# Pairs of units with one f and one scan, PSUM banks named one by one, and another order of issue in a recurrence-plus-highway kernel

## The chip, the core and the metric

The kernel runs on one core of one Trainium2 chip. The metric is the device time of one execution in microseconds (us). The core has a matrix engine (PE, with its weight loads PEld), a vector engine (DVE), a scalar engine (ACT), a GpSimd engine (POOL) and a sync engine (SP), which here issues nearly all transfers. Each engine works through its own queue in program order. PE writes only to PSUM, which has 8 banks of 512 fp32 columns; DVE and ACT read PSUM, POOL does not.

## What is computed

Four sequences of 6336 tokens with 256 features pass through a gated recurrence; the result of all 25344 tokens then passes through a highway layer.

```
sig = 1 / (1 + exp(-f_logit))
f = lower_bound + (1 - lower_bound) * sig
i = 1 - f
h = 0                                  # for each of the 4 sequences
for t in range(6336):
    h = f[:, t] * h + i[:, t] * x[:, t]
    y[:, t] = h

H = max(y @ w_h, 0)
T = 1 / (1 + exp(-(y @ w_t + b_t)))
out = T * H + (1 - T) * y
```

Inputs and output are fp32; the two input arrays and the output are 25.95 MB each.

## The kernel before

The tokens are cut into 28 units of whole blocks of 128 tokens (`parts`, L42): two units of 2 blocks, one of 4, twenty-three of 8, one of 4, one of 2. Features are two halves of 128 (`h`, `m`). For each unit the steps are these; the letter is the one used in the order.

- `l`, `x` (L235): load logits and x, up to 1 MB each, tokens on partitions.
- `u` (L247, ACT): u = sigmoid(-logits), 2048 columns for a unit of 8 blocks. The gate is f = 1 - (1 - lower_bound) u.
- `b` (L255, POOL, or DVE where the token ends in `v`): products u times x in bf16, in two pieces of 1024 columns.
- `i` (L262, PE): transposes of u, 8 of 128 columns, so that features lie on partitions and time along the columns; `f` (L273 on ACT, L271 on DVE): the gate, read from PSUM.
- `p` (L282, PE): transposes of the products, two bf16 values as one fp32 word; `s` (L299, DVE): the scan along time, y = f*y + b, which reads the products in PSUM and carries on from the last column of the unit before. A scan is cut where a sequence begins.
- `z`, `g` (L311 and, without a new weight load, L113; PE): the two matrix products, in pieces of 512 columns. The weights are scaled by 1 - lower_bound, because the scan leaves that factor out.
- `t` (L324, ACT): the sigmoid of z; `d` (L328, DVE): max(g, -(1 - lower_bound) y); `e` (L334, POOL or DVE): d = d * t.
- `o` (L347 and L348, PE): y times a diagonal plus d, transposed back to tokens on partitions, 4 blocks at a time; `c` (L357 on ACT, L355 on DVE): the copy from PSUM; `w` (L362): the store of 512 KB.

Once at the start come the loads of the weights (`wt`, `wh`), the small parameters (`pc`, `cc`, `dg`) and the scaling of the weights (`WT`, `WH`, DVE). `k*16` and `k*4` are matmuls on zeros whose result nobody reads (L124, L113).

The string `order` (L48 to L97) sets the order of everything: each token calls one of the functions, and instructions keep that order on each engine and in the queue of each engine, SP's included. The number behind the colon names the buffer. PSUM is cut into two buffers of one bank (`a0`, `a1`: uT and bT) and three of two banks (`b0` to `b2`: z, g, op). SBUF has six buffers for `l`, six for `x`, four each for `u`, `f`, `y`, `d` and `o`, three for `t` and `bv`. A transfer waits on SP until its buffer is free or its data is there, and the transfers behind it wait with it. `shared` (L176) makes the first POOL step behind a DVE step of the kind `b`, `e`, `dg`, `WT` or `WH` wait for that DVE step.

Of the kernel before, what the change touches and what calls it, by code (L numbers as in the profile page):

```python
# [11 lines left out]
FP32 = mybir.dt.float32  # L12
# [7 lines left out]
def kernel(  # L20
# [10 lines left out]
    nc = tc.nc  # L31
# [10 lines left out]
    parts = [2] * 2 + [4] + [8] * 23 + [4] + [2]  # L42
    units, at = [], 0
    for nb in parts:
        units.append((nb, at, {2: (0, 1), 4: (0, 1, 2), 8: (0, 2, 4)}[nb], {2: (0, 256, 512), 4: (0, 512, 1024), 8: (0, 1024, 2048)}[nb]))
        at += nb * P
    assert at == B * S
    order = """  # L48
l0:0 l1:1 x0:0 l2:2 wh wt x2:1 x1:2 u0:0 l3:3 pc:0 u2:1 x3:3 cc u1:2 l4:0 i0.1:0 x4:4 dg b0.0v:0 i0.0:1 k*16:1 l5:4
f0.0v:0 x5:5 f0.1v:1 WH p0.0:0 WT p0.1:1 k*4:0 s0.1:0 l6:5 x6:0 i2.0:1 b1.0:0 s0.0 f2.0:1 i1.0:0 z0.1:0 f1.0v:0 g0.1:1  # L50
g0.0:2 d0.1:0 b2.0:1 d0.0 p1.1:1 t0.1:0 i1.1:0 z0.0:0 k*4:1 b2.1 f1.1v:2 s1.1:1 p1.0:0 t0.0 p2.0:1 s1.0 e0.0 s2.0:2
z1.1:0 e0.1 u3:0 i2.1:0 z1.0:1 g1.1:2 b3.0:0 d1.1:1 p2.1:1 f2.1:0 g1.0:2 s2.1 t1.0:0 b3.1v d1.0 i3.0:0 k*4:1 t1.1
f3.0:1 g2.0:0 o0.0:1 i3.1:0 e1.1 e1.0 u4:1 d2.0:0 f3.1:0 p3.0:1 c0.0:0 s3.0:0 b4.1:1 z2.1:2 k*4:0 o1.0:0 b4.0 p3.1:0
# [19 lines left out]
f16.0:2 b16.1:1 l19:0 d13.1 b16.0 t13.0 p15.0:1 c12.0:2 i17.1:0 x19:3 f17.1:1 z14.1:1 g14.0:0 p15.1:0 e13.1 s15.0:2
o12.1:2 b17.1:0 u18:2 d14.0:0 z14.0:0 p16.0:1 b17.0 l20:1 t14.1:1 t14.0 c12.1:0 s15.1 g14.1:1 i16.1:0 s16.0:1 z15.0:0
f16.1:0 e13.0v w12.0 z15.1:2 d14.1 e14.0 t15.0:2 p16.1:0 i17.0:1 e14.1 w12.1 t15.1 o13.0:0 b18.1:1 f17.0:2 c13.0:1
w13.0 l21:2 x20:0 u19:0 g15.0:2 s16.1 b18.0 p17.0:1 d15.0:1 o13.1:1 g16.0:0 i18.1:0 c13.1:3 z16.1:2 g15.1:1 f18.1:0
s17.0:3 w13.1 t16.1:0 i19.1:0 d16.0:2 p17.1:1 f19.1:2 o14.0:2 u20:1 o14.1:0 b19.0:0 l23:0 c14.1:0 i18.0:0 w14.1 b19.1
# [12 lines left out]
x27:3 o22.0:2 t23.1:1 b26.0:0 s24.1 e21.0v t21.1 c22.0:1 z23.0:0 p25.0:0 e21.1 o22.1:1 t23.0 z24.1:2 u27:0 i26.0:1  # L90
g24.0:0 s25.0:0 c22.1:2 f26.0:0 b26.1 z24.0:1 d24.0:0 p25.1:1 t24.1:2 i26.1:0 w20.1 e23.0 t24.0 o21.0:2 e23.1 g24.1:0
f26.1:1 c21.0:0 e24.0 o21.1:1 s25.1 p26.0:0 c21.1:3 p26.1:1 d24.1 s26.1:3 z25.1:2 w22.0 t25.1:0 g25.1:0 w22.1 w21.0
d25.1:1 o23.0:1 w21.1 s26.0 o23.1:2 i27.1:1 c23.0:1 z25.0:0 b27.0:0 w23.0 c23.1:0 g26.0:1 g25.0:2 t25.0 e24.1v d26.0:2
d25.0 i27.0:0 e25.1 e25.0v w23.1 f27.0:0 z26.1:0 o24.0:1 f27.1:1 p27.0:0 p27.1:1 z26.0:2 s27.0:2 s27.1 t26.1:1 c24.0:2
o25.0:0 t26.0 g26.1:1 w24.0 o24.1:2 d26.1 z27.0:1 c24.1v:0 c25.0:1 t27.0:0 o25.1:0 c25.1:3 e26.0 g27.0:1 d27.0:0 e26.1
o26.0:2 w25.0 w24.1 z27.1:1 t27.1 e27.0v c26.0:2 w25.1 w26.0 g27.1:0 d27.1 e27.1v o27.0:0 c27.0:1 w27.0
"""  # L97

    NU = len(units)
# [3 lines left out]
    st = [dict() for _ in range(NU)]  # L103
# [15 lines left out]
    extra = [0]  # L119

    def busy(t):
        for k in range(extra[0]):
            if k == 0:
                pin(nc.tensor.matmul(t[:, :512], zeros[:, :P], zeros, start=True, stop=True))  # L124
            else:
                pin(again(t[:, :512], zeros[:, :P], zeros, True, True))

    def one_bank(slot, dtype, name):
        t = ps.tile([P, NB * P], dtype, tag=f"a{slot}", name=name)
        busy(t.bitcast(FP32))  # L130
        return t

    def two_banks(slot, name):
        t = ps.tile([P, NB * P], FP32, tag=f"b{slot}", name=name)
        busy(t)
        return t
# [13 lines left out]
    for _ in range(8):  # L150
        nc.tensor.matmul(once["idle"][:, :512], zeros[:, :P], zeros, start=True, stop=True)
# [251 lines left out]
```

## Time and profile before

| what | value |
|---|---|
| runs | 213.06, 212.94, 210.38 us; median 212.94 |
| the profiled execution, span of its instructions | 209.0 us |
| transferred | 78.67 MB, mean 376 GB/s |
| ACT, POOL busy | 191.1 us (91%), 176.2 us (84%) |
| last load of x issued on SP | at 174.40 us |
| SP's own waiting | 130.2 us for ACT copies, in 42 waits |

The profile gives a span from the first to the last instruction of one execution; the time of the runs has 1.4 to 4.1 us beside such a span. Busy times are unions of instruction records, and neighbouring records on DVE and ACT overlap by some 0.1 us, so start-to-start distances are the better price of one more or one less instruction. A matmul's record is longer than the distance to the next matmul, since matmuls are pipelined.

### The profile page before, as it was taken

How to read it: one execution, taken by the hardware profiler on the slowest of the kernel's cores; microseconds unless marked ns; L12 is line 12 of the kernel's file. 1: busy time of each engine (PE TensorE's matmuls, PEld its weight loads, DVE VectorE, ACT ScalarE, POOL GpSimd, SP SyncE). 2: the span in 40 equal slices, each digit the busy share in tenths (PEclk: the TensorE clock that was granted, in tenths of full speed). 3: DMA queues.
4: the chain of work that ended last, by engine and by line, in shares of the span. 5: the costliest groups of instructions: out<-in, count | busy, mean ns of one | idle time of the engine just before them, and what ended most of it. 6: DMA issues, size and time to landing. Idle time of an engine off the chain costs nothing.

```text
span 209.0 us, 4656 instructions
## 1 busy us (share of the span) xinstructions
PE 197.0 (94%) x1852; PEld 135.3 (65%) x1852; DVE 194.8 (93%) x159; ACT 191.1 (91%) x185; POOL 176.2 (84%) x101
## 2 busy tenths in 40 slices
PE   7989998999899999899999999999999999999991
PEld 2446575686576577558676667575677776777680
DVE  0789999999999999999999999999999999999971
ACT  4368999999999999999999999999999999997972
POOL 3076998989997887997999899788999999989740
PEclk9999999999999999999999999999999999999999
DMA  6999999999999999999999999999999999655567
GB/s 174 367 419 423 416 417 421 416 423 372 422 408 351 387 427 413 416 417 412 410 420 416 423 418 424 408 425 412 426 421 400 379 405 341 267 204 201 199 278 279
DMA packets 15980, 78.67 MB, mean 376 GB/s; under 512 B 1748, under 2 KB 2264, under 8 KB 10072
## 3 DMA queue, kind: packets, MB, share of 16 engines
q1 hardware_dynamic: 15952, 78.39, 93.6%
q8 instruction: 14, 0.23, 0.5%
q14 instruction: 6, 0.05, 0.1%
q10 hardware_dynamic: 8, 0.00, 0.0%
HBM read 52.43 MB, written 25.95 MB: 375 GB/s over the span
## 4 chain that ended last, share of the span: by engine, by line
PE 50%; DVE 14%; ACT 12%; DMA 9%; issue 8%; POOL 4%; SPq 1%; DVEq 0%; ACTq 0%; POOLq 0%
DVE y L299 10%; PE op L347 7%; PE op L348 7%; PE z L311 7%; PE bT L282 6%; DMA x<-in_x_dram 6%; PE z L113 6%; PE g L311 6%; PE g L113 5%; PE uT L262 5%; ACT f L273 4%; DVE d L328 4%; ACT o L357 4%; POOL bv L255 3%; DMA l<-in_f_logit_dram 3%
## 5 line engine op out<-in xcount | busy, mean ns | idle before, releaser
L255 POOL TENSOR_TENSOR bv<-u,x 128x1024 bf16<-128x1024 f16 (+1 forms) x51 | 103.2, 2046 | 17.2 <-DVE y L299 9.3
L299 DVE TENSOR_TENSOR_SCAN y<-f,y,bT 128x1024 bf16<-128x1024 f16 (+5 forms) x54 | 106.8, 1991 | 1.0 <-PE bT L282 0.3
L334 POOL TENSOR_TENSOR d<-d,t 128x1024 bf16<-128x1024 bf16 (+2 forms) x39 | 73.0, 1888 | 7.8 <-DVE d L334 4.1
L328 DVE SCALAR_TENSOR_TENSOR d<-y,ncc,g 128x1024 bf16<-128x1024 bf16 (+2 forms) x56 | 62.9, 1140 | 1.6 <-PE g L311 1.0
L324 ACT ACTIVATE t<-z,bt 128x1024 bf16<-128x1024 f32 (+2 forms) x56 | 58.4, 1075 | 2.3 <-PE z L311 1.9
L273 ACT ACTIVATE f<-uT,ncc 128x1024 f16<-128x1024 f16 (+2 forms) x51 | 56.4, 1120 | 3.5 <-PE uT L262 3.2
L247 ACT ACTIVATE u<-l 128x2048 f16<-128x2048 f32 (+2 forms) x28 | 49.6, 1774 | 5.1 <-DMA l<-in_f_logit_dram 4.5
L357 ACT COPY o<-op 128x1024 f32<-128x1024 f32 (+1 forms) x48 | 48.9, 1047 | 2.3 <-PE op L348 1.7
L347 PE MATMUL op<-diag,y 128*128 128x128 f16 x396 | 49.4, 219 | 1.1 <-DVE d L328 0.6
L348 PE MATMUL op<-ident_b,d 128*128 128x128 bf16 x396 | 49.4, 219 | 0.1
L348 PEld LDWEIGHTS <-d 128*128 128x128 bf16 x396 | 44.0, 113 | 4.6 <-issue 1.6
L347 PEld LDWEIGHTS <-y 128*128 128x128 bf16 x396 | 44.2, 113 | 1.8
L311 PE MATMUL z<-y,w_sb 128*128 128x512 bf16 (+1 forms) x112 | 39.5, 367 | 0.5 <-ACT o L357 0.5
L311 PE MATMUL g<-y,w_sb 128*128 128x512 bf16 (+1 forms) x112 | 39.2, 367 | 0.1
L113 PE MATMUL z<-y,w_sb 128*128 128x512 bf16 x92 | 34.9, 379 | 0.0
L113 PE MATMUL g<-y,w_sb 128*128 128x512 bf16 x92 | 34.8, 379 | 0.0
L282 PE MATMUL bT<-ident_f,bv 128*128 128x128 f32 x198 | 31.4, 277 | 2.7 <-POOL bv L255 1.1
L262 PEld LDWEIGHTS <-u 128*128 128x128 f16 x396 | 26.3, 98 | 11.2 <-issue 4.8
L262 PE MATMUL uT<-ident_h,u 128*128 128x128 f16 x396 | 31.1, 220 | 2.2 <-ACT f L273 1.0
L311 PEld LDWEIGHTS <-w_sb 128*128 128x128 f16 x224 | 21.4, 98 | 15.5 <-DVE y L299 0.4
L282 PEld LDWEIGHTS bT<-ident_f,bv 128*128 128x128 f32 x198 | 22.6, 141 | 11.5 <-POOL bv L255 2.3
L113 PEld LDWEIGHTS <-w_sb 128*128 128x128 f16 x184 | 18.0, 98 | 16.2 <-issue 1.8
(36 smaller groups left out, 61.9 us busy)
## 6 DMA issues: line engine op xcount, KB each, us to landing
out_dram<-o SPq DMA_DIRECT2D x48, 512.0 KB, 7.0
l<-in_f_logit_dram SPq DMA_DIRECT2D x23, 1024.0 KB, 11.1
x<-in_x_dram SPq DMA_DIRECT2D x23, 1024.0 KB, 10.8
l<-in_f_logit_dram SPq DMA_DIRECT2D x2, 512.0 KB, 6.9
x<-in_x_dram SPq DMA_DIRECT2D x2, 512.0 KB, 7.0
l<-in_f_logit_dram SPq DMA_DIRECT2D x3, 256.0 KB, 3.2
x<-in_x_dram SPq DMA_DIRECT2D x3, 256.0 KB, 7.3
out_dram<-o SPq DMA_DIRECT2D x3, 256.0 KB, 6.7
```

The lines of the kernel that those rows point to most:

```text
L113: return pe.add_instruction(mybir.InstMatmult(name=nc.get_next_instruction_name(), start_tensor_calc=start, stop_tensor_calc=stop, tile_si ...
L255: shared(pin(e.tensor_mul(st[n]["bv"][:, a:c].rearrange("p k d j -> p k j d"), st[n]["u"][:, 2 * a:2 * c].rearrange("p (k j) d -> p k j d" ...
L262: pin(nc.tensor.transpose(uT[:, j * P:(j + 1) * P], st[n]["u"][:, j, h * P:(h + 1) * P], ident_h))
L273: pin(nc.scalar.activation(to, of, AF.Identity, scale=ncc[:, h:h + 1], bias=1.0))
L282: pin(nc.tensor.transpose(words[:, k:k + g * (P - 1) + 1:g], pair, ident_f))
L299: pin(nc.vector.tensor_tensor_scan(y[:, c:e], st[n]["f", h][:, c:e], st[n]["bT", h][:, c:e], 0.0 if fresh else carry[h], op0=ALU.mult, op1 ...
L311: pin(nc.tensor.matmul(p[:, a:e], w, half(n, "y", ki)[:, a:e], start=ki == 0, stop=ki == NH - 1))
L324: pin(nc.scalar.activation(half(n, "t", m), st[n]["z", m][:, :tokens(n)], AF.Sigmoid, bias=bt[:, m:m + 1]))
L328: pin(nc.vector.scalar_tensor_tensor(half(n, "d", m), half(n, "y", m), ncc[:, m:m + 1], st[n]["g", m][:, :tokens(n)], op0=ALU.mult, op1=AL ...
L334: shared(pin(e.tensor_mul(st[n]["d"][:, a:c], st[n]["d"][:, a:c], st[n]["t"][:, a:c])), not eng)
L347: pin(nc.tensor.matmul(o, half(n, "y", h)[:, cols], diag[:, h], start=True, stop=False))
L348: pin(nc.tensor.matmul(o, half(n, "d", h)[:, cols], ident_b, start=False, stop=True))
```

## The change

Fourteen of the 8-block units become seven pairs: the unit list is now 21 units, each with one or two parts (`subs`). A pair loads, takes `u` and `b`, and is transposed (`i`, `p`) part by part, as before; but it has one `f` and one scan per half of the features, over 2048 columns. `z`, `g`, `t`, `d`, `e`, `o`, `c` and `w` still go by 8 blocks or less, numbered by a further index `q`. The three places where a sequence begins inside a unit all lie in pairs now.

PSUM is one tensor of 8 banks, and each token names its bank or its two neighbouring banks (`:5`, `:45`, also `:12`). Transposes of a pair take two banks, one for each part. `B` and `E` are `b` and `e` of both pieces in one instruction. The first DVE or POOL step on the shared port is no longer held back by `dg`, `WT` and `WH`.

The order is new throughout. Counted over the whole order, against before:

| step | before | after |
|---|---|---|
| scans, without the extra cuts at the beginnings of sequences | 46 of 1024, 4 of 512, 6 of 256 columns | 14 of 2048, 18 of 1024, 4 of 512, 6 of 256 |
| f on ACT | 45 of 1024, 4 of 512, 2 of 256 | 14 of 2048, 17 of 1024, 4 of 512, 3 of 256 |
| f on DVE | 1 of 1024, 4 of 256 | 1 of 1024, 3 of 256 |
| c on DVE | 3 of 1024 | 1 of 1024, 1 of 512 |
| b on DVE | 1 of 1024, 1 of 512 | 1 of 2048, 1 of 512 |
| e on DVE | 15 of 1024, 2 of 256 | 2 of 2048, 11 of 1024, 1 of 512, 1 of 256 |
| u, t, d, z, g, i, p, o, w, l, x | as many columns as after | as many columns as before |
| idle matmuls in the order | 49, the last in unit 11 | 49, the last between the two scans of unit 3 |

SBUF now has five buffers for `l`, five for `x`, six for `y` (of 2048 columns for one half, where there were four of 2048 for both halves), and the `f` buffers are twice as wide. At the start the first load of x goes ahead of the second of logits, `wt` ahead of `wh`, the first scan ahead of `WT`, and the products of unit 0 ahead of `cc`. The logits of the last unit are loaded in the middle of the kernel (`l20.0`), and its first gate, `f20.1`, is made before unit 16 is scanned.

```diff
-    parts = [2] * 2 + [4] + [8] * 23 + [4] + [2]
+    parts = [(2,), (2,), (4,), (8,), (8,), (8,), (8,), (8, 8), (8, 8), (8, 8), (8, 8), (8, 8), (8, 8), (8, 8), (8,), (8,), (8,), (8,), (8,), (4,), (2,)]
...
+l0.0:0 u0.0:0 pc:0 k*4:1 x0.0:0 b0.0.0v:0 p0.0.0:1 i0.0.1:2 cc dg f0.1v:0 p0.0.1:0 i0.0.0:3 l1.0:1 u1.0:1 l2.0:2
+u2.0:2 s0.1:0 f0.0v:0 i1.0.1:4 i1.0.0:5 k*16:6 wt WT f1.0:1 i2.0.0:0 s0.0:1 z0.0.1:1 x1.0:1 b1.0.0:1 p1.0.1:2 p1.0.0:3
+wh WH z0.0.0:5 k*4:6 f1.1:2 i2.0.1:4 g0.0.1:6 f2.0:3 x2.0:2 t0.0.0:0 s1.1:2 g0.0.0:0 l3.0:3 s1.0:3 g1.0.1:2 z1.0.1:3
...
+d7.1.1:0 B8.1:0 p8.1.1:67 u9.1:3 g7.0.1:01 d7.0.1 o5.0.1:45 c5.0.1:1 B8.0:2 p8.0.1 s8.1:4 z7.0.1:23 t7.0.1:1 z7.1.1:01
+w4.0.1 z7.0.0:45 t7.1.1:2 t7.0.0 p8.1.0:23 p8.0.0 E6.0 o6.0.1:01 c6.0.1:0 o6.0.0:67 c6.0.0:3 b9.0.0:1 z7.1.0:45
+i9.0.0:01 b9.0.1 i9.1.0 b9.1.0:0 g7.1.0:67 t7.1.0 b9.1.1 l10.1:3 s8.0:5 l10.0:4 f9.0:1 i9.1.1:45 e7.0.1 u10.1:2 w5.0.1
+d7.1.0 e7.0.0 g8.1.1:23 d8.1.1:1 x10.1:3 g8.1.0:01 d8.1.0 i9.0.1 f9.1:2 w5.0.0 g8.0.0:67 p9.1.1:23 p9.0.1 i10.1.0:01
...
+e18.0.0 e18.0.1v p20.0.1:4 c17.0.1:2 w17.0.1 d19.0.1:3 z19.0.1:5 o18.0.1:67 z19.0.0:0 s20.0:4 s20.1:5 t19.0.1:1
+c18.0.1:0 t19.0.0 g19.0.0:1 w18.0.1 o18.0.0:23 c18.0.0:1 e19.0.1 d19.0.0 g20.0.1:4 z20.0.0:0 z20.0.1:1 t20.0.1:0
+e19.0.0v t20.0.0 o19.0.0:67 w18.0.0 c19.0.0:3 g20.0.0:2 w19.0.0 d20.0.1:1 d20.0.0 e20.0.1 e20.0.0v o20.0.0:0 c20.0.0:2
+w20.0.0
...
+    psum = ps.tile([P, BANKS * BANK], FP32, tag="psum", name="psum")
...
+    def do_f(eng, slot, n, h):
+        N, subs = tokens(n), units[n][1]
+        f = sb([P, 2 * NB * P], FP16, "f", slot)
+        to, of = f[:, :N], st[n]["uT", h].all(N)
...
+            to = to.rearrange("c (s p j) -> c s p j", s=len(subs), j=subs[0])
+            of = of.rearrange("c (s j p) -> c s p j", s=len(subs), j=subs[0])
...
+    def do_s(eng, slot, n, h):
+        y = sb([P, 2 * NB * P], BF16, "y", slot)
+        st[n]["y", h] = y
         for fresh, c, e in pieces(n):
...
+            data = st[n]["bT", h].part(c, e)
+            pin(nc.vector.tensor_tensor_scan(y[:, c:e], st[n]["f", h][:, c:e], data,
                                              0.0 if fresh else carry[h], op0=ALU.mult, op1=ALU.add))
```

More of the change, by code (lines that the diff above doesn't have):

```diff
@@ L73 @@
[L73 to L77, printed above, removed]
@@ L118 @@
     zeros = sb([P, 512], BF16, "zeros")
[L119 to L136, printed above, removed]
     warm = sb([P, 64], FP32, "warm")
@@ L148 @@
     nc.vector.memset(zeros, 0.0)
-    once["idle"] = two_banks(2, "idle")
-    for _ in range(8):
-        nc.tensor.matmul(once["idle"][:, :512], zeros[:, :P], zeros, start=True, stop=True)
+    for _ in range(6):
+        pin(nc.tensor.matmul(psum[:, 7 * BANK:], zeros[:, :P], zeros, start=True, stop=True))
     prm = sb([2 * NH, P], FP32, "prm")
@@ L190, in do_pc @@
     def do_pc(slot):
-        once["prmT"] = ps.tile([P, 2 * NH], FP32, tag=f"b{slot}", name="prmT")
+        once["prmT"] = Banks(slot).one(0)[:, :2 * NH]
         pin(nc.tensor.transpose(once["prmT"], prm, ident_f[:2 * NH, :2 * NH]))
@@ L223, in do_WH, with do_k @@
                                                op0=ALU.mult, op1=ALU.add))
-            last = pin(nc.vector.tensor_scalar(w_sb[:, 0, h, rest], w_raw[:, 0, h, rest], cc[:, h:h + 1], None,
+            pin(nc.vector.tensor_scalar(w_sb[:, 0, h, rest], w_raw[:, 0, h, rest], cc[:, h:h + 1], None,
                                                op0=ALU.mult))
-        shared(last, False)
-    def rows(full, n, j0, j1):
-        at = units[n][1]
+    def do_k(slot, times):
+        out = Banks(slot).one(0)
+        for k in range(times):
+            if k == 0:
+                pin(nc.tensor.matmul(out, zeros[:, :P], zeros, start=True, stop=True))
+            else:
+                pin(again(out, zeros[:, :P], zeros, True, True))
@@ L331, in do_e @@
[L331 to L341 removed]
+                    pin(again(p.part(a, e), w, data, ki == 0, ki == NH - 1))
```

336 lines of the change are left out of this document (185 added, 151 removed).

## The prediction

> **What bounds the kernel now.** I read the page first: busy shares, then the slices of the span.
>
> ```profile
> PE 197.0 (94%) x1852; PEld 135.3 (65%) x1852; DVE 194.8 (93%) x159; ACT 191.1 (91%) x185; POOL 176.2 (84%) x101
> ...
> DVE  0789999999999999999999999999999999999971
> ...
> PEclk9999999999999999999999999999999999999999
> DMA  6999999999999999999999999999999999655567
> GB/s 174 367 419 423 416 417 421 416 423 372 422 408 351 387 427 413 416 417 412 410 420 416 423 418 424 408 425 412 426 421 400 379 405 341 267 204 201 199 278 279
> ```
>
> Four engines and the transfers are all above 80%, so shares alone decide nothing. DVE has a full digit from the fourth slice to the 38th. The transfers are full too, but only to about 178 us (34 of 40 slices); then they fall to half, because the loads are through and only stores remain. The table by stage and the waits settle it:
>
> ```profile
> 0.00:10.00 10.00, 8.81 (x33) 3.80 (x34) 3.94 (x16) 3.75 (x5) 1.62 (x11) 1.00 0.81 263
> 100.00:120.00 20.00, 19.83 (x192) 13.93 (x191) 19.76 (x16) 20.00 (x19) 19.31 (x11) 1.00 1.02 418
> 200.00:209.00 9.00, 4.32 (x62) 3.63 (x59) 3.39 (x6) 3.96 (x6) 1.69 (x2) 0.96 0.76 300
> ...
> DVE ncc L196 <- PE prmT L192: 3.9, 1, 3.9
> DVE w_sb L222 <- DMA w_raw<-in_moe_w_h_dram: 1.3, 1, 1.3
> ```
>
> Columns of the first three: stretch, its length, then PE, PEld, DVE, ACT, POOL busy, granted clock, DMA share, GB/s. DVE is idle 209.0 - 194.8 = 14.2 us. Of these, 6.1 lie in the first 10 us and 5.6 in the last 9, so about 2.5 us are left for the 190 us between. The two longest waits of DVE are both at the start. **DVE's queue is the bound**: what it has less to do comes off the end, as long as its inputs come as punctually as now. ACT follows closely (91%, 20.00 of 20.00 in the second stretch).
>
> **DVE's work.** Prices are start-to-start, from a stretch where DVE never waits (start, length, engine, line):
>
> ```profile
> 183.45 0.66 DVE L334 TENSOR_TENSOR d<-d,t 128x1024 bf16<-128x1024 bf16 x1
> 184.04 2.33 DVE L299 TENSOR_TENSOR_SCAN y<-f,y,bT 128x1024 bf16<-128x1024 f16 x1
> 186.29 1.25 DVE L328 SCALAR_TENSOR_TENSOR d<-y,ncc,g 128x1024 bf16<-128x1024 bf16 x1
> 187.47 2.33 DVE L299 TENSOR_TENSOR_SCAN y<-f,y,bT 128x1024 bf16<-128x1024 f16 x1
> 189.72 1.25 DVE L328 SCALAR_TENSOR_TENSOR d<-y,ncc,g 128x1024 bf16<-128x1024 bf16 x1
> ...
> 193.40 1.27 DVE L299 TENSOR_TENSOR_SCAN y<-f,y,bT 128x512 bf16<-128x512 f16 x1
> 194.59 0.89 DVE L334 TENSOR_TENSOR d<-d,t 128x1024 bf16<-128x1024 bf16 x1
> ```
>
> A scan of 1024 columns costs 2.25 us (184.04 to 186.29), one of 512 costs 1.19 (193.40 to 194.59): 1.06 per 512 columns and 0.13 fixed. A scan of 2048 is then 4.37 against 4.50 for two, and fourteen pairs of scans become one each: 14 x 0.13 = 1.8 us. By the records' full lengths (2.33 and 1.27) the fixed part is 0.21, the saving 2.9; this is the upper end. No scan over two banks is in the trace. If the second bank costs as much as a new instruction, the saving is nothing: the lower end. I take 1.8, from rows that show when the next instruction really starts.
>
> The Trainium skill, page "VectorE: DVE Perf Modes", section "The TRN2 errata — SBUF-src ops pay a fixed extra latency per instruction", says that a large tile pays the fixed latency once and many small ones each time, about 150 cycles at 0.96 GHz by its measurement; an estimate from that is 14 x 0.156 = 2.2 us. No row here shows such a pair yet; the rows above put the fixed part at 0.13 to 0.21.
>
> The other moves on DVE and ACT, from the view that groups by form:
>
> ```profile
> L255 DVE TENSOR_TENSOR bv<-u,x 128x1024 bf16<-128x1024 f16 x1 | 1.3, 1337 | 0.0
> L355 DVE COPY o<-op 128x1024 f32<-128x1024 f32 x3 | 3.6, 1204 | 0.1
> L271 DVE TENSOR_SCALAR f<-uT,ncc 128x256 f16<-128x256 f16 x4 | 1.8, 480 | 0.4 <-PE uT L262 0.4
> L334 DVE TENSOR_TENSOR d<-d,t 128x256 bf16<-128x256 bf16 x2 | 0.6, 292 | 0.2
> L273 ACT ACTIVATE f<-uT,ncc 128x1024 f16<-128x1024 f16 x45 | 52.7, 1185 | 1.3 <-PE uT L262 1.1
> L273 ACT ACTIVATE f<-uT,ncc 128x512 f16<-128x512 f16 x4 | 2.9, 713 | 1.9 <-PE uT L262 1.8
> L357 ACT COPY o<-op 128x1024 f32<-128x1024 f32 x45 | 47.1, 1077 | 2.0 <-PE op L348 1.7 <-ACT t L324 0.2
> ```
>
> DVE's copies fall from three of 1024 columns to one of 1024 and one of 512 (taken at half): 1.5 x 1.20 = -1.8. One f of 256 goes: -0.5. One more b of 1024 comes: +1.3. One e of 512 comes (between the rows 0.66 and 0.29, about 0.4) and one of 256 goes: +0.1. Together -0.9; each record shortened by the overlap of 0.08 changes this by 0.1. The merged B and E on DVE save under 0.1 each. **DVE: 1.8 + 0.9 = 2.7 us less**; between 0.9 and 3.9.
>
> **ACT** saves the fixed part of fourteen f: 1185 - 2 x (1185 - 713) = 241 ns each, 3.4 us. It takes over 1.5 copies (1.6) and one f of 256 (about 0.5). That is 1.3 us less, so ACT, at 191.1 busy, comes closer to DVE at 194.8 - 2.7 = 192.1. POOL loses one b and some fixed parts and stays the least loaded.
>
> **The start.** DVE begins with nothing to do until the small parameters arrive, then with a hole before the weights:
>
> ```profile
> 0.74 0.86 SPq L235 DMA_DIRECT2D l<-in_f_logit_dram  x2
> 2.58 0.43 SPq L188 DMA_DIRECT2D w_raw<-in_moe_w_h_dram  x1
> 3.86 0.63 ACT L247 ACTIVATE u<-l 128x512 f16<-128x512 f32 x1 [1.00 <-DMA l<-in_f_logit_dram]
> 5.01 0.16 DVE L196 TENSOR_SCALAR ncc<-prmT 128x2 f32<-128x2 f32 x1 [3.88 <-PE prmT L192]
> 6.08 0.72 DVE L255 TENSOR_TENSOR bv<-u,x 128x512 bf16<-128x512 f16 x1
> 6.69 0.87 DVE L271 TENSOR_SCALAR f<-uT,ncc 128x256 f16<-128x256 f16 x2
> 8.83 0.35 DVE L222 SCALAR_TENSOR_TENSOR w_sb<-w_raw,cc,ndiag 128x128 f16<-128x128 f32 x1 [1.27 <-DMA w_raw<-in_moe_w_h_dram]
> 10.28 1.26 DVE L299 TENSOR_TENSOR_SCAN y<-f,bT 128x256 bf16<-128x256 f16 x2
> ```
>
> u of unit 0 is ready at 4.5 (3.86 + 0.63). The changed order issues x of unit 0 second, so it should be there by then, and its b (0.72, 0.61 to the next start) runs in the idle time before 5.01: 0.6 gained. Then the first scan goes ahead of the weights: 0.6 of work falls into the 1.27 us hole, in front of an instruction that still waits for the fifth transfer, as now. The two first scans and weights would be done at about 11.0 instead of 11.54. The hole being partly filled twice over is not certain, so I take 1.2 us for the start; from nothing to 2.0. Two things speak against it: all 49 idle matmuls of the order now stand ahead of the second scan of unit 3, where 36 stand ahead of the scans of unit 4 before, and PE has to get through them before it finishes the transposes of unit 4; and the weights for the other product land two transfers later. Both are hidden if PE would have waited there anyway, and cost up to 13 x 0.22 = 2.9 us if not (0.22 us a matmul, rows below).
>
> **The transfers.** SP's order is new, loads go further ahead of their use, and two buffers fewer hold them. I price that at nothing: 78.67 MB at 418 GB/s are 188 us, from about 2 us on, and the loads are 20 us and more ahead of the end now (last full DMA slice at 178 us). DVE waits for no x or logits after the start. If that cover goes, a late load of 1 MB costs 2.5 us (1 MB at 418 GB/s) each time.
>
> **The tail.**
>
> ```profile
> 198.24 1.38 DVE L299 TENSOR_TENSOR_SCAN y<-f,y,bT 128x256 bf16<-128x256 f16 x2
> 199.49 1.02 ACT L357 COPY o<-op 128x1024 f32<-128x1024 f32 x1 [0.21 <-ACT t L324]
> 205.04 0.59 ACT L357 COPY o<-op 128x512 f32<-128x512 f32 x1 [0.31 <-ACT o L357]
> ```
>
> From the end of the last scan (199.62) to the end of the span are 9.4 us. In that time four copies of 1024 columns and the last of 512 are made now. The changed order leaves three and the one of 512 behind its last scan, and u and f of the last unit are long done. One copy less is 1.0 us on ACT, beside DVE's share of the work, so I count 0.6; from nothing to 1.5.
>
> **Sum:** 2.7 + 1.2 + 0.6 = 4.5 us off the span of 209.0, giving 204.5. The runs lie 1.4 to 4.1 above that span, the median 3.9; from the median, 212.9 - 4.5 = **208.4 us**.
>
> **The rivals.**
>
> *More comes off.* All terms at their upper ends: 3.9 + 2.0 + 1.5 = 7.4, 205.5 us. For it: DVE idles only 2.5 us in the middle, so it can use what it saves. Against: ACT saves 1.3 only.
>
> *ACT becomes the bound.* DVE's gain ends where ACT's work ends; 1.3 us come off and start and tail give nothing: 211.6 us. For it: 20.00 busy of 20.00. Against: ACT starts earlier on unit 1 as well.
>
> *PSUM is short (slower).* A scan of a pair holds two banks for 4.4 us, twice the time and twice the banks of now, and the pair's two scans stand back to back (`s8.1`, `s8.0`) with no `d` between them to empty a g bank. Two more banks hold the next products. PE is left with four, and the t and c of ACT alone to empty them. For it: PE had three two-bank buffers for z, g and op and used them at 94%. Against: the order gives PE z, o and i of earlier units in that time. PE idles 12.0 us now, 5.9 of it in the first 10 and last 9, so it can lose 6.1 us before it ends later, and 2 more with the gains at start and tail (1.8, rounded up). If it stands L per pair, the end moves by 7 L - 8.1: later than now from L = 1.2 us, over 2% later from 1.8. With L = 2, 5.9 us: 218.8 us.
>
> *PE slows after a pause.* The trace shows a matmul of 512 columns at half rate at the start and at full rate later:
>
> ```profile
> 2.02 0.15 PEld L151 LDWEIGHTS <-zeros 128*128 128x128 bf16 x1 [0.28 <-issue]
> 2.44 0.15 PEld L151 LDWEIGHTS <-zeros 128*128 128x128 bf16 x1 [0.28 <-issue]
> ...
> 38.08 0.38 PE L311 MATMUL z<-y,w_sb 128*128 128x512 bf16 x1
> 38.30 0.38 PE L113 MATMUL z<-y,w_sb 128*128 128x512 bf16 x1
> ```
>
> 0.42 against 0.22 us, though the granted clock reads 1.00 in both stretches. The change has no idle matmul after unit 3, where now there are some up to unit 11. If each pair made PE pause long enough to lose 1.5 us to the half rate, 10.5 - 8.1 = 2.4: 215.3 us. The Trainium skill, page "TensorE: Matmul & The Clock Gate", section "Part 1: The HAM clock gate (the "warmup" mystery)", has the array fall to half its clock after about 3.4 us of idling; the rates above agree with two such states, but no row here shows a fall in the middle.
>
> **How the numbers follow.** A measurement of this kernel can tell about 2% from no change, 4.3 us. My forecast has 0.52; its own range is 206 to 211, and 0.33 of it lies below 208.7, 0.19 above. More comes off: 0.10. ACT: 0.10. PE slows: 0.04, within 2%. PSUM is short: 0.24, nearly all beyond 2%. Faster 0.33 + 0.10 = 0.43; within 2% 0.19 + 0.10 + 0.04 = 0.33; slower 0.24. The range runs from 204.5, a little beyond the upper ends of the terms, to 217, which leaves out somewhat over half of the PSUM case.
>
> **What would show it.** Right: scans of 2048 columns at about 4.4 us, DVE busy near 192 with under 3 us idle between 10 us and the tail, DVE's first scan near 7 us, PE waiting in short pieces only. Wrong: DVE waiting for bT or g behind each pair (PSUM), PE idle well over 12 us, a scan of 2048 above 4.5 us, or waits of DVE or ACT for transfers in the middle. If ACT is full and DVE shows gaps of under 1 us everywhere, ACT is the bound.

## The result and the profile after

| | before | after |
|---|---|---|
| median of six runs each on one chip | 212.38 us (210.38 to 214.93) | 208.71 us (208.07 to 208.94) |
| span of the profiled execution | 209.0 us | 207.1 us |
| DVE busy, idle in that span | 194.8, 14.2 us | 192.8, 14.3 us |

The ratio is 0.9849, with a 95% interval of 0.9812 to 0.9886: 1.5% faster, 3.7 us. The forecast was 208.4 us. Two things stand out before any experiment. The medians differ by 3.7 us, the two profiled spans only by 1.9. And the runs of before lie 4.6 us apart, those of after 0.9.

The page of the changed kernel, first the busy times, then the slices of the span:

```profile
PE 194.7 (94%) x1850; PEld 135.0 (65%) x1850; DVE 192.8 (93%) x141; ACT 190.9 (92%) x173; POOL 171.9 (83%) x90
...
DVE  2799989999999999999999979999999999999971
...
DMA  6999999999999999999999999999999999934576
```

DVE has a digit in the first slice already, and a 7 in slice 24. DVE has 2.0 us less work. Where its idle time lies is read from the table by stretch (stretch, length, then PE, PEld, DVE, ACT, POOL busy, granted clock, DMA share, GB/s). First before, then after:

```profile
0.00:20.00 20.00, 17.29 (x103) 9.18 (x104) 12.99 (x30) 10.69 (x14) 8.44 (x17) 1.00 0.92 342
20.00:180.00 160.00, 155.40 (x1487) 107.99 (x1484) 158.90 (x109) 158.45 (x146) 149.19 (x73) 1.00 1.01 408
180.00:209.00 29.00, 24.30 (x268) 18.14 (x266) 22.89 (x22) 21.92 (x28) 18.62 (x12) 0.99 0.57 224
```

```profile
0.00:20.00 20.00, 18.54 (x116) 10.19 (x117) 14.55 (x29) 12.71 (x18) 7.09 (x17) 1.00 0.92 344
20.00:180.00 160.00, 153.51 (x1495) 108.05 (x1494) 157.13 (x93) 157.29 (x133) 146.78 (x65) 1.00 1.01 411
180.00:207.10 27.10, 22.60 (x242) 16.73 (x240) 21.15 (x21) 20.90 (x25) 18.04 (x10) 1.00 0.56 221
```

DVE's idle time goes from 7.0 to 5.5 us in the first 20, from 1.1 to 2.9 in the middle, and from 6.1 to 6.0 in the rest. Between these two executions the gain at the start is paid back in the middle, and the 1.9 us are DVE's work alone. The timeline of after shows DVE's longest waits behind 25 us (start, length, engine, line, operation, in brackets the idle time ahead and what ended it):

```profile
28.19 2.35 DVE L320 TENSOR_TENSOR_SCAN y<-f,y,psum 128x1024 bf16<-128x1024 f16 x1 [0.62 <-ACT f L301]
35.08 1.28 DVE L363 SCALAR_TENSOR_TENSOR d<-y,ncc,psum 128x1024 bf16<-128x1024 bf16 x1 [0.36 <-PE psum L145]
121.28 4.85 DVE L363 SCALAR_TENSOR_TENSOR d<-y,ncc,psum 128x1024 bf16<-128x1024 bf16 x4 [1.17 <-PE psum L145]
201.93 0.48 DVE L363 SCALAR_TENSOR_TENSOR d<-y,ncc,psum 128x256 bf16<-128x256 bf16 x1 [1.06 <-ACT t L356]
```

The third stands behind the second scan of pair 11 (the digit 7): the first `d` there needs a `g` of that same pair, and no other work covers the time. The other six pairs show no such wait.

### The profile page after: what moved, and what is told of

The parts are those of the page before. It is cut to its first block, busy times and chain, and to the rows that moved or that the text cites. A ratio compares the mean times of both kernels' runs of the same rounds, so it can differ in the third digit from the quotient of the medians.

```text
span 207.1 us, 4606 instructions
## 1 busy us (share of the span) xinstructions
PE 194.7 (94%) x1850; PEld 135.0 (65%) x1850; DVE 192.8 (93%) x141; ACT 190.9 (92%) x173; POOL 171.9 (83%) x90
## 4 chain that ended last, share of the span: by engine, by line
PE 48%; DVE 17%; ACT 16%; DMA 11%; issue 4%; POOL 2%; SPq 1%; DVEq 0%; ACTq 0%
PE psum L333 13%; PE psum L145 11%; DMA l<-in_f_logit_dram 11%; DVE y L320 10%; PE psum L393 6%; DVE d L363 6%; PE psum L394 6%; ACT f L301 6%; PE psum L286 6%; PE psum L311 5%; ACT u L262 4%; ACT t L356 3%; ACT o L405 2%; POOL bv L277 2%; DVE f L299 1%
## 5 line engine op out<-in xcount | busy, mean ns | idle before, releaser
L277 POOL TENSOR_TENSOR bv<-u,x 128x1024 bf16<-128x1024 f16 (+2 forms) x44 | 99.8, 2293 | 18.3 <-ACT f L301 7.4
L320 DVE TENSOR_TENSOR_SCAN y<-f,y,psum 128x1024 bf16<-128x1024 f16 (+6 forms) x40 | 103.7, 2614 | 1.0 <-ACT f L301 0.6
L377 POOL TENSOR_TENSOR d<-d,t 128x1024 bf16<-128x1024 bf16 (+3 forms) x35 | 71.7, 2063 | 11.4 <-ACT t L356 6.1
L333 PE MATMUL psum<-y,w_sb 128*128 128x512 bf16 (+1 forms) x224 | 77.4, 367 | 3.0 <-ACT f L301 1.9
L145 PE MATMUL psum<-y,w_sb 128*128 128x512 bf16 x184 | 69.7, 379 | 0.7 <-DVE y L320 0.7
L363 DVE SCALAR_TENSOR_TENSOR d<-y,ncc,psum 128x1024 bf16<-128x1024 bf16 (+2 forms) x56 | 62.6, 1147 | 3.4 <-PE psum L145 1.5
L356 ACT ACTIVATE t<-psum,bt 128x1024 bf16<-128x1024 f32 (+2 forms) x56 | 56.3, 1038 | 2.6 <-PE psum L145 1.7
L301 ACT ACTIVATE f<-psum,ncc 128x1024 f16<-128x1024 f16 (+3 forms) x38 | 50.9, 1365 | 1.6 <-PE psum L286 1.6
L393 PE MATMUL psum<-diag,y 128*128 128x128 f16 x396 | 48.8, 219 | 0.6 <-ACT f L301 0.4
L394 PE MATMUL psum<-ident_b,d 128*128 128x128 bf16 x396 | 48.6, 219 | 0.8 <-DVE d L377 0.8
L311 PE MATMUL psum<-ident_f,bv 128*128 128x128 f32 x198 | 29.3, 276 | 1.3 <-POOL bv L277 0.8
L311 PEld LDWEIGHTS psum<-ident_f,bv 128*128 128x128 f32 x198 | 22.4, 141 | 7.1 <-POOL bv L277 2.1
```

Source lines behind the costliest of these rows:

```text
L145: return pe.add_instruction(mybir.InstMatmult(name=nc.get_next_instruction_name(), start_tensor_calc=start, stop_tensor_calc=stop, tile_si ...
L277: shared(pin(e.tensor_mul(st[n]["bv", s][:, a:c].rearrange("p k d j -> p k j d"), st[n]["u", s][:, 2 * a:2 * c].rearrange("p (k j) d -> p ...
L301: pin(nc.scalar.activation(to, of, AF.Identity, scale=ncc[:, h:h + 1], bias=1.0))
L311: pin(nc.tensor.transpose(words[:, k:k + g * (P - 1) + 1:g], pair, ident_f))
L320: pin(nc.vector.tensor_tensor_scan(y[:, c:e], st[n]["f", h][:, c:e], data, 0.0 if fresh else carry[h], op0=ALU.mult, op1=ALU.add))
L333: pin(nc.tensor.matmul(p.part(a, e), w, data, start=ki == 0, stop=ki == NH - 1))
```

## The experiments

Each run has the kernel before beside it on the same chip; its medians there were 211.57, 212.24 and 212.40 us in the three groups in which they ran: the work and the start; the transfers and the first try at unit 4; the last four. These medians differ by 0.8 us, so a difference of that size between kernels of different groups is not resolved.

### The work on DVE and on ACT

**The changed kernel again.** 

> The changed kernel once more, unaltered, as the measure for the other three. Both theories: about 208.7 us, with runs within 0.5 us of each other.

Measured: 208.73 us (207.72 to 209.0), profiled span 205.9, DVE busy 192.9. The span moves by 1.2 us between the two profiled executions (207.1 and 205.9), so the experiments below are compared with a median of 208.7.

**The scan of a pair in two again**, at 1024 columns:

```diff
-        cuts = [0] + [c - at for c in firsts if at < c < at + N] + [N]
+        inner = [c - at for c in firsts if at < c < at + N] + ([NB * P] if N > NB * P else [])
+        cuts = [0] + sorted(inner) + [N]
```

> The changed kernel, but each scan of a pair is cut at column 1024 again: 14 scans more on DVE, same order, same f. Theory 1 (DVE's queue is the bound): 14 x 0.13 = 1.8 us more than the changed kernel, about 210.5. Theory 2 (the gain came from somewhere else, DVE has room): at most 0.5 more.

Measured: 212.08 us (211.37 to 213.19), 3.35 more, with DVE at 195.5 busy. The whole advantage is gone by this edit alone: what DVE loses reaches the end one to one, and a cut costs more than I had priced. Of the loss 2.6 us are busy time; the rest are gaps of 0.04 to 0.10 us behind the first scan of each such two. The same place in the two timelines, uncut and cut (the x counts instructions run together):

```profile
65.17 8.85 DVE L320 TENSOR_TENSOR_SCAN y<-f,y,psum 128x2048 bf16<-128x2048 f16 x2
73.94 3.73 DVE L363 SCALAR_TENSOR_TENSOR d<-y,ncc,psum 128x1024 bf16<-128x1024 bf16 x3
```

```profile
65.75 9.34 DVE L321 TENSOR_TENSOR_SCAN y<-f,y,psum 128x1024 bf16<-128x1024 f16 x4
75.00 3.74 DVE L364 SCALAR_TENSOR_TENSOR d<-y,ncc,psum 128x1024 bf16<-128x1024 bf16 x3
```

Start to start, two scans of 2048 take 8.77 us, 4.39 each (forecast 4.37); four of 1024 take 9.25. That is 0.24 us a cut here and up to 0.32 at other places, and 14 x 0.24 = 3.4: the cuts cover the whole loss. In before a scan of 1024 took 2.25 to the next start, that is 0.13 fixed. The difference between the two arrangements: in before the two halves of the features take turns, while here a scan begins with the last value of the one directly ahead of it. This run itself shows it: a scan of 1024 takes 2.36 to 2.45 us to the next scan's start at the 14 places where that scan begins with its last value, and 2.26 to 2.30 where it doesn't.

**f of a pair in two again**, one instruction per 1024 columns:

```diff
-        to, of = f[:, :N], st[n]["uT", h].all(N)
...
+        for s, nb in enumerate(subs):
+            a = sum(subs[:s]) * P
+            to = f[:, a:a + nb * P].rearrange("c (p j) -> c p j", j=nb)
+            of = st[n]["uT", h].part(a, a + nb * P).rearrange("c (j p) -> c p j", j=nb)
```

> The changed kernel, but each f of a pair is two instructions of 1024 columns again: 14 instructions more on ACT, 2.2 to 3.4 us of ACT work by the two prices of the prediction. Theory 1 (DVE is the bound, ACT has a little room): at most 0.7 us more. Rival (ACT is the bound as well now): 2 us more or over.

Measured: 209.21 us (208.8 to 210.05), with ACT at 192.4 busy in place of 190.9. 1.5 us more work on ACT cost 0.5. ACT is close behind DVE but not the bound, since then all 1.5 would have come through; the merged `f` saved 0.11 us apiece (1.5 / 14), not the 0.24 that I took from the two sizes of before.

### The start

**The old order of the first transfers and of DVE's first steps**, the rest as changed:

```diff
-l0.0:0 u0.0:0 pc:0 k*4:1 x0.0:0 b0.0.0v:0 p0.0.0:1 i0.0.1:2 cc dg f0.1v:0 p0.0.1:0 i0.0.0:3 l1.0:1 u1.0:1 l2.0:2
-u2.0:2 s0.1:0 f0.0v:0 i1.0.1:4 i1.0.0:5 k*16:6 wt WT f1.0:1 i2.0.0:0 s0.0:1 z0.0.1:1 x1.0:1 b1.0.0:1 p1.0.1:2 p1.0.0:3
-wh WH z0.0.0:5 k*4:6 f1.1:2 i2.0.1:4 g0.0.1:6 f2.0:3 x2.0:2 t0.0.0:0 s1.1:2 g0.0.0:0 l3.0:3 s1.0:3 g1.0.1:2 z1.0.1:3
+l0.0:0 u0.0:0 pc:0 k*4:1 l1.0:1 x0.0:0 l2.0:2 wh wt x2.0:2 x1.0:1 cc dg b0.0.0v:0 p0.0.0:1 i0.0.1:2 f0.1v:0 p0.0.1:0
+i0.0.0:3 u1.0:1 u2.0:2 f0.0v:3 i1.0.1:4 i1.0.0:5 k*16:6 WH WT s0.1:0 f1.0:1 i2.0.0:0 s0.0:1 z0.0.1:1 b1.0.0:1 p1.0.1:2
+p1.0.0:3 z0.0.0:5 k*4:6 f1.1:2 i2.0.1:4 g0.0.1:6 f2.0:3 t0.0.0:0 s1.1:2 g0.0.0:0 l3.0:3 s1.0:3 g1.0.1:2 z1.0.1:3
```

> The changed kernel with the old kernel's order of transfers at the start (l of unit 1 ahead of x of unit 0, weights w_h ahead of w_t, x of units 2 and 1 before the first scan) and with the first scan behind both weights on DVE. Theory 1 (what DVE gains at the start lasts to the end): 1.2 us more, from 0.8 to 1.6. Rival (units 3 to 5 are paced by the arrival of their loads, so that the start gains nothing): at most 0.3 more.

Measured: 209.27 us (208.74 to 211.71), 0.5 more. At the first scan of unit 3 this kernel is 1.25 us behind the first profile of the changed kernel (21.81 against 20.56 us), at the first of unit 4 only 0.55 (28.74 against 28.19): in the changed kernel that scan stands 0.62 us for `f4.0`, which waits on ACT behind `u5`, and `u5` for its load. In that execution the start is won as priced, and half of it is lost to the next late input. The second profile of the changed kernel shows that this isn't so in every execution. The load of unit 5 in the first (207.1 us), then that load and the scan of unit 4 in the second (205.9 us):

```profile
25.07 1.91 ACT L262 ACTIVATE u<-l 128x2048 f16<-128x2048 f32 x1 [0.77 <-DMA l<-in_f_logit_dram]
```

```profile
23.92 1.91 ACT L262 ACTIVATE u<-l 128x2048 f16<-128x2048 f32 x1 [0.20 <-DMA l<-in_f_logit_dram]
27.04 2.35 DVE L320 TENSOR_TENSOR_SCAN y<-f,y,psum 128x1024 bf16<-128x1024 f16 x1
```

There the scan of unit 4 starts 1.15 us earlier than in the first, without a wait, and the span is 1.2 shorter: nearly all of the difference between the two executions arises ahead of this scan, where the first inputs land.

The timelines of this run and of the changed kernel's first profile show a price that I had not listed. With the change the scaling of the weights (DVE) falls beside a product on POOL; with the old start it doesn't. First the changed kernel, DVE's rows and POOL's, then the old start:

```profile
10.22 0.72 DVE L230 SCALAR_TENSOR_TENSOR w_sb<-w_raw,cc,ndiag 128x128 f16<-128x128 f32 x1 [0.21 <-DMA w_raw<-in_moe_w_h_dram]
10.87 0.27 DVE L232 TENSOR_SCALAR w_sb<-w_raw,cc 128x128 f16<-128x128 f32 x1
...
9.63 1.17 POOL L277 TENSOR_TENSOR bv<-u,x 128x512 bf16<-128x512 f16 x1 [7.40 <-ACT f L301]
```

```profile
8.38 0.35 DVE L230 SCALAR_TENSOR_TENSOR w_sb<-w_raw,cc,ndiag 128x128 f16<-128x128 f32 x1 [0.65 <-DMA w_raw<-in_moe_w_h_dram]
8.64 0.28 DVE L232 TENSOR_SCALAR w_sb<-w_raw,cc 128x128 f16<-128x128 f32 x1
```

The first scaling takes 0.65 us to the next start beside POOL and 0.26 without; the next one starts right behind the end of POOL's product (10.80 us). The change had dropped the hold by which the first POOL step waits for such a DVE step.

### The transfers

**The kernel before again.** 

> The kernel before once more, unaltered, to see where its runs differ: six runs so far lie between 210.4 and 214.9 us, six of the changed kernel between 208.1 and 208.9. Theory A (its loads arrive with little to spare, so that a slow transfer reaches DVE): a profile with a span above 210 shows more waits for l or x, or for steps behind them, than the one of 209.0. Rival (a general slowness of the run): all instructions or the clock a little slower, no new waits.

Measured: 212.25 us median. The execution profiled here has a span of 210.1 us at the same work on DVE (195.0). Among its waits are some that the first profile of before lacks; one chain of them, on DVE and on POOL:

```profile
139.01 4.58 DVE L299 TENSOR_TENSOR_SCAN y<-f,y,bT 128x1024 bf16<-128x1024 f16 x2 [0.56 <-PE bT L282]
...
136.97 4.28 POOL L255 TENSOR_TENSOR bv<-u,x 128x1024 bf16<-128x1024 f16 x2 [1.46 <-DMA x<-in_x_dram]
```

POOL stands for a load, and two steps later DVE for the products. Two more waits of DVE for products cost 0.36 us each, at 168.36 and 172.24 us, behind a wait of ACT for logits of 0.59 at 166.89. The loads of before arrive just in time, and in some executions a little late. After issues them further ahead: at the same rate of transfer in the middle (408 and 411 GB/s) they land later behind their issue, and in neither of its two profiles does ACT, POOL or DVE wait for a load behind 26 us. The page's transfer lines, issue to landing, before and then after:

```profile
l<-in_f_logit_dram SPq DMA_DIRECT2D x23, 1024.0 KB, 11.1
```

```profile
l<-in_f_logit_dram SPq DMA_DIRECT2D x23, 1024.0 KB, 14.6
```

**The old order with its loads deeper**: in before, each load moves up to right behind the step that frees its buffer, past one to five stores; at the start some also pass the loads of the weights.

```diff
 z4.0:1 s5.0 i7.0:1 d4.0 b6.1
+x9:0 l10:2
 c3.1:0 p6.0:0 s6.0:3 e4.1 z5.1:2 w3.1
...
 p6.1:1 f7.1:1
-x9:0
 c3.0:1 e4.0v w3.0 e5.1
-l10:2
 u8:0
```

> The kernel before, where only l and x tokens move: each goes up to right behind the step that frees its buffer, past 1 to 5 stores. Theory A (late issue costs the old kernel): 1 to 2.5 us less than the kernel before and runs within 1 us. Rival (depth in the queue does nothing for the time): within 0.5 us of it. A third outcome, stores held up behind waiting loads: over 1 us slower.

Measured: 246.93 us (245.64 to 248.86), 34.7 more. SP's own waits, in total, times, longest:

```profile
SPq L236 <- ACT u L248: 69.9, 16, 10.5
SPq L236 <- POOL bv L256: 32.7, 7, 8.9
```

A load whose buffer isn't free yet holds SP, and all stores behind it. Then `o` buffers stay full: ACT's copies wait 24.7 us for stores. The third of the expected outcomes holds, at far more than its price. 8.6 us of DVE's waits are at the start, for weights that now land later; that part is not the stores' doing. So the run doesn't tell whether a harmless deeper order would have helped the kernel before.

**The new order with its loads two stores later**, 30 of 38 loads from unit 8 on:

```diff
 d8.1.1:1
-x10.1:3
 g8.1.0:01 d8.1.0 i9.0.1 f9.1:2 w5.0.0
...
 d8.0.0:2 w6.0.0
+x10.1:3
 w6.0.1
```

> The changed kernel, where from unit 8 on each load (30 of 38) is issued two stores later, as far as its first reader allows; nothing else moves. Theory A: 1 us more or over, with a wider spread of the runs, and waits of ACT or POOL for l and x in the profile. Rival: within 0.5 us of the changed kernel.

Measured: 231.96 us (229.81 to 233.38), ratio to before 1.089 (1.083 to 1.096). The waits of ACT and POOL for loads, in the longest of its runs, which is the profiled one:

```profile
ACT u L261 <- DMA l<-in_f_logit_dram: 18.0, 11, 6.7
...
POOL bv L276 <- DMA x<-in_x_dram: 17.2, 6, 6.1
```

Two stores in one queue cost 23 us. A misplaced load can cost more than everything else in this change gained.

### Waits that the changed kernel still has

**f of unit 4 ahead of u of unit 5**, and its `p` ahead of `i` of unit 5, to end the wait of 0.62 us at 28.19:

```diff
-u5.0:1 i5.0.1:2 p4.0.0:1 B5.0:2 i5.0.0:3 z3.0.0:45 f4.0:3
+f4.0:3 u5.0:1 p4.0.0:1 i5.0.1:2 B5.0:2 i5.0.0:3 z3.0.0:45
```

> The changed kernel with two tokens moved: the f of unit 4, second half, ahead of u of unit 5 on ACT, and the transposes p of unit 4 ahead of i of unit 5 on PE. In the profile DVE stood 0.62 us there, because u of unit 5 waited for its logits. Theory 1 (DVE is the bound): 0.5 us less. Rival (the time comes back at a later wait): no change within 0.2.

Measured: 209.99 us (209.35 to 210.81), 1.3 more. The wait is gone and another is there, on PE and then DVE:

```profile
29.08 1.07 PE L286 MATMUL psum<-ident_h,u 128*128 128x128 f16 x16 [1.14 <-ACT u L262]
...
31.91 1.28 DVE L363 SCALAR_TENSOR_TENSOR d<-y,ncc,psum 128x1024 bf16<-128x1024 bf16 x1 [1.30 <-PE psum L145]
```

PE works in order: it stands for `u5`, now later, and the `g` of unit 3 is queued behind.

**The same, with z and g of unit 3 ahead of the transposes of unit 5 on PE:**

```diff
-u5.0:1 i5.0.1:2 p4.0.0:1 B5.0:2 i5.0.0:3 z3.0.0:45 f4.0:3 f5.1:2 f5.0:1 g3.0.0:67 z3.0.1:23
+f4.0:3 u5.0:1 p4.0.0:1 z3.0.0:45 g3.0.0:67 i5.0.1:2 B5.0:2 i5.0.0:3 f5.1:2 f5.0:1 z3.0.1:23
```

> f of unit 4 goes ahead of u of unit 5 on ACT, and on TensorE the products of unit 4 and the last z and g of unit 3 go ahead of the transposes of unit 5, which must wait for that u. Theory (the earlier attempt failed because TensorE, in order, stood at the transposes of unit 5 with the g of unit 3 behind them): both waits of DVE near 28 to 32 us fall below 0.3 us, 0.6 us come off, 208.1. Rival (the load of unit 5 and u behind it pace the stretch): the wait comes back as one for f or bT of unit 5 by about 38 us, and the time is within 0.2 us.

Measured: 210.46 us (209.7 to 210.82), 1.75 more. Again the wait moved:

```profile
28.04 1.06 PE L286 MATMUL psum<-ident_h,u 128*128 128x128 f16 x16
...
30.92 0.38 PE L145 MATMUL psum<-y,w_sb 128*128 128x512 bf16 x1 [0.63 <-ACT f L301]
...
31.56 1.04 PE L311 MATMUL psum<-ident_f,bv 128*128 128x128 f32 x8
...
32.20 2.35 DVE L320 TENSOR_TENSOR_SCAN y<-f,y,psum 128x1024 bf16<-128x1024 f16 x1 [1.88 <-PE psum L311]
```

The second `z` of unit 3 needs banks 2 and 3, which `f` of unit 5 must empty first; that `f` is later now, and the products of unit 4 (L311) stand behind the `z` on PE. The rival is right in that the wait comes back, but for products of unit 4 and sooner than it said, and the time is not within its 0.2 us: neither outcome holds.

**Cover behind pair 11**: a product `e` of 0.66 us moves on DVE from ahead of the pair's second scan to behind it.

```diff
-e10.1.0v
 e10.1.1 s11.1:5
+e10.1.0v
...
-o10.1.0:23 c10.1.0:1
 c10.0.0:2 g11.1.1:01 d11.1.1:0 g11.0.1:67 d11.0.1:1 e9.1.0
-g11.0.0:23
+g11.0.0:45 o10.1.0:23 c10.1.0:1
```

> One product of unit 10 on DVE (0.66 us) moves from ahead of the second scan of pair 11 to behind it, and the output products that read it move behind the g of pair 11, which changes banks. Theory (behind the scan of a pair DVE stands for g, because no other work covers it): the wait at that place falls from 1.17 to about 0.5 us, and about 0.7 us come off, 208.0. Rival (a later wait, for ACT or a load, takes it up again): DVE's first d of pair 11 is 0.6 earlier but the end is within 0.2 us.

Measured: 210.64 us (210.18 to 211.4), 1.9 more. POOL first, then DVE:

```profile
119.44 6.38 POOL L277 TENSOR_TENSOR bv<-u,x 128x1024 bf16<-128x1024 f16 x3 [3.10 <-DVE d L377]
...
119.80 1.28 DVE L363 SCALAR_TENSOR_TENSOR d<-y,ncc,psum 128x1024 bf16<-128x1024 bf16 x1 [0.58 <-PE psum L145]
...
126.35 4.48 DVE L320 TENSOR_TENSOR_SCAN y<-f,y,psum 128x2048 bf16<-128x2048 f16 x1 [1.20 <-PE psum L311]
...
135.20 2.29 DVE L377 TENSOR_TENSOR d<-d,t 128x1024 bf16<-128x1024 bf16 x2
```

The wait behind the scan fell from 1.17 to 0.58, as the theory says. But POOL's next product is held back until that `e` of DVE is done, by the hold named in the section on the kernel before. It stood 3.10 us; the products of pair 12 came late (1.20), and POOL, shifted, then ran beside the first of two `e` of DVE, which took 2.29 us together where after has 1.26. 0.6 + 0.2 + 1.2 + 1.0 against 1.2 is 1.8 us more.

**The last g in a free bank**, ahead of the output products of units 18 and 19:

```diff
 g20.0.1:4
+g20.0.0:5
 z20.0.0:0 z20.0.1:1 t20.0.1:0 e19.0.0v t20.0.0 o19.0.0:67 w18.0.0 c19.0.0:3
-g20.0.0:2
 w19.0.0 d20.0.1:1 d20.0.0
```

> The last g of the last unit goes to a bank that is free after z of unit 19 and stands right behind its sister on TensorE; before, it stood behind the output products of units 18 and 19 and in a bank that ACT's copy had to empty. Theory (DVE's queue sets the end, the last d waits 1.06 us for g): that wait falls below 0.2 us, last d 0.9 earlier, and 0.3 to 1.0 us come off, about 208.1 against 208.7, since ACT's last copies follow. Rival (the end is ACT's copies or the last stores): the wait goes and the time stays within 0.2 us of the changed kernel's.

Measured: 208.46 us (207.65 to 209.0), 0.25 less, which is within the spread. The wait of the last `d` is gone and the last product and copy follow earlier. First this kernel (DVE, DVE, ACT), then the changed kernel in its second profile, whose last scans lie within 0.01 us of this one's:

```profile
199.29 0.87 DVE L363 SCALAR_TENSOR_TENSOR d<-y,ncc,psum 128x256 bf16<-128x256 bf16 x2
200.79 0.50 DVE L377 TENSOR_TENSOR d<-d,t 128x256 bf16<-128x256 bf16 x1 [0.63 <-ACT t L356]
...
201.99 0.59 ACT L405 COPY o<-psum 128x512 f32<-128x512 f32 x1 [0.17 <-PE psum L394]
```

```profile
200.82 0.48 DVE L363 SCALAR_TENSOR_TENSOR d<-y,ncc,psum 128x256 bf16<-128x256 bf16 x1 [1.06 <-ACT t L356]
...
202.40 0.59 ACT L405 COPY o<-psum 128x512 f32<-128x512 f32 x1 [0.76 <-ACT o L405]
```

The last copy starts 0.41 us earlier, yet the spans are 206.0 and 205.9: the last store took 2.5 us to land in place of 2.0. In this pair of profiles the end belongs to the last stores, as the rival said, and DVE's wait there costs nothing.

**All three edits together.** 

> The three edits together. If DVE's queue is the bound at all three places, the gains add: 0.6 + 0.7 + 0.6 = 1.9 us, 206.8. If each is taken up by another engine or by the loads, under 0.5 us, 208.2 or more.

Measured: 212.76 us (212.05 to 213.93). The single results add up to 208.7 - 0.25 + 1.75 + 1.9 = 212.1: a loss, where the second forecast had a gain of under 0.5. No version beyond the changed kernel was found that beats it by more than the spread.

## Why the prediction was right, and where it was not

**DVE is the bound: right.** 3.35 us come back when its scans are cut, with nothing else altered. ACT as the bound in its place is ruled out by the split `f`: 1.5 us more work on ACT cost 0.5.

**Scans, 1.8 us: right for this comparison.** A scan of 2048 takes 4.39 us. By the view that groups by line, the records of all scans sum to 113.8 us in place of 116.8; less the overlap of 0.08 us on 14 instructions, that is 1.9. Against the kernel before the merging is worth that; inside the new order it is worth 3.4, since cuts are dearer where scans of one half stand in a row.

The Trainium skill, page "VectorE: DVE Perf Modes", section "The TRN2 errata — SBUF-src ops pay a fixed extra latency per instruction", gives about 150 cycles at 0.96 GHz for an instruction, from which I had estimated 0.156 us. The runs show 0.13 and 0.24 to 0.32 for the same scan, so the fixed cost depends on whether the next scan needs its last value, which that section does not distinguish.

**DVE's work, 2.7 us: 2.0.** Each record counted only up to the start of the next one, the terms of the sum held: the scans fell by 1.9 us (113.3 to 111.3), the copies by 1.7, `f` by 0.4 and `e` by 0.4, and `b` rose by 1.4, together 3.0 less. The step that failed is the one that put the steps whose number stays at nothing. The 56 `d` became 0.65 us dearer (60.15 to 60.80), and the scaling of the weights 0.38 (1.30 us, 10.22 to 11.52, in place of 0.92), since the first scaling now runs beside a POOL product; its price came from rows in which POOL was idle. Why `d` is dearer stays open. The product of 2048 columns took 2.72 us where 2.43 stands in the run with the old start, but its price, twice 1.34, already held that.

**The start, 1.2 us: 0.5 at the end.** The step "hidden if PE would have waited there anyway" was not the failure; the gain reached unit 3 in full and then, in one of the two profiles, met the load of unit 5.

**The tail, 0.6 us: some 0.1.** DVE's idle time behind 180 us fell from 6.1 to 6.0. The stretch behind the last scan did become 1.3 us shorter (9.4 to 8.1), but 1.2 of that is DVE's own work, which is counted already. The step was wrong to let a copy less on ACT move the end, which waits for the last stores.

**ACT, 1.3 us less: 0.2.** Busy went from 191.1 to 190.9; the fixed part of `f` was mis-sized (0.11 us in place of 0.24), with little effect on the time, as the split `f` shows.

**The transfers, nothing: the mis-sized term that saved the sum.** The three terms above came to 2.0 + 0.5 + 0.1 = 2.6, not 4.5, and the sum was taken from a median whose excess over the profile I left standing. That the forecast lies within 0.3 us of the result is partly luck: what these terms lacked came from a term put at nothing. In the runs whose span was recorded a run is 1.7 to 1.9 us longer than its own span, not 1.4 to 4.1, so the median run of before has a span of 210.6, and 195.0 of it is DVE's work: 15.6 idle. After it is 207.0, with 14.1 idle. So of the 3.7 us about 2.1 are work and 1.5 idle time. The idle time includes waits behind before's late loads: the profile of 209.0 us has two waits of POOL for a load behind 26 us (the longer 0.59), that of 210.1 six of POOL and ACT (the longest 1.46), the two of after none. That late loads occur in before is thus shown; that they make up its spread and most of the 1.5 us is argued from the narrow spread of after, since no run gives before a harmless deeper order.

**PSUM is short: at one pair of seven.** 1.17 us at pair 11, not 2 us at each. PE idles 12.4 us, 0.4 more than before, and hid the rest. **PE slows after a pause: not in this kernel.** Its longest pause behind 20 us is 1.29, and a matmul of 512 columns behind it has the record of full rate, 0.38 us, where the first idle matmul of the order has 0.61:

```profile
4.06 0.61 PE L239 MATMUL psum<-zeros 128*128 128x512 bf16 x1
...
55.40 0.38 PE L333 MATMUL psum<-y,w_sb 128*128 128x512 bf16 x1 [1.29 <-ACT f L301]
```

The mechanism itself exists, and two of the runs above show it. In the old order with deeper loads (mean granted clock 0.94) PE pauses for 4.23 us; matmuls of 512 columns then run 0.43 us apart for 3 us, and 0.22 apart from there on:

```profile
62.15 0.59 PE L312 MATMUL g<-y,w_sb 128*128 128x512 bf16 x1 [4.23 <-ACT o L358]
62.53 0.63 PE L114 MATMUL g<-y,w_sb 128*128 128x512 bf16 x1
62.96 0.63 PE L312 MATMUL g<-y,w_sb 128*128 128x512 bf16 x1
...
66.04 0.38 PE L114 MATMUL z<-y,w_sb 128*128 128x512 bf16 x1
66.26 0.38 PE L312 MATMUL z<-y,w_sb 128*128 128x512 bf16 x1
```

In the run with late loads (0.97) the rate halves behind pauses of 2.1, 2.5 and 6.6 us (at 135.10, 114.50 and 187.81 us) and not behind one of 1.84 (at 170.21). What the half rate added to the time of these two runs is not separated. The Trainium skill, page "TensorE: Matmul & The Clock Gate", section "Part 1: The HAM clock gate (the "warmup" mystery)", names about 3.4 us of idling for the fall to half rate. The changed kernel's pauses are shorter, which agrees; the run with late loads shows the fall behind 2.1 us already, and here the measurement decides.

## What to carry to other kernels

Where one engine's queue sets the end, count its work, and ask of each piece which other engine will run beside it in its new place. Where runs spread more than their profiles explain, look for inputs that arrive just in time, and price the place of every load in the queue: misplaced loads cost 23 and 35 us here, where the merged scans were worth 3.4. Removing one wait in such an order often only moves it, as in three of the four attempts here, since each engine's order, each bank and each hold passes it on; follow the moved step through all of them first.

## What the runs showed of the hardware

- The fixed cost of a scan on DVE is not one number: 0.13 us in before, where the halves take turns, and 0.24 to 0.32 when the next scan begins with its last value (0.24 above; at pair 11 two scans of 1024 take 4.71 us where one of 2048 takes 4.39).
- DVE instructions on SBUF operands stand while a POOL product runs: a scaling of 0.26 us took 0.65, and a pair of products 2.29 us in place of 1.26. The instruction behind the scaling started 0.07 us after POOL's had ended. A DVE product of 1024 columns, 0.67 us alone, takes about 0.55 us and the time that POOL's product goes on beside it: 0.84 with 0.29 (after, 33.88 us), 0.89 with 0.35 (before, 194.59), 1.68 with 1.14 (the run with cover behind pair 11, 135.20).
- Behind the first microseconds, PE's matmuls fell to half rate (0.43 in place of 0.22 us apart at 512 columns) behind every pause of 2.1 us and more in these traces, and behind none of up to 1.84.
- The profile's granted clock reads 1.00 in the first 20 us, where the first matmuls of 512 columns start 0.43 us apart, against 0.22 later.
